# The last residual sum of a transformer kernel prepared ahead, and its last token tile worked in two column halves

## The chip, the cores and the metric

One core of a Trainium2 chip runs the kernel. The metric is the time of one execution on the device in microseconds (us), quoted as the median of several runs. Each run also has a state, fast or slow. PE is TensorE, DVE is VectorE, ACT is ScalarE, POOL is GpSimd, SP is SyncE, which here only issues transfers. The span is the time from the first to the last instruction in a trace. The views round it to 0.1 us; where this text gives the end of a span to 0.01 us, the figure is from the packed trace, which keeps it to the ns (1245.400 us before).

## The reference

Two layers, each a sliding-window attention and a feed-forward block (FFN), on x of 2048 tokens by 1024 columns in bfloat16. What matters here is the end of each FFN:

```python
def _B_ref(x, w1, b1, w2, b2):
    h = jnp.einsum("bsd,df->bsf", x, w1) + b1      # 1024 -> 3584
    h = _gelu(h)
    return jnp.einsum("bsf,fd->bsd", h, w2) + b2   # 3584 -> 1024
...
x = x + _B_ref(_layernorm(x, axis=-1), B_w1, B_b1, B_w2, B_b2)
```

## The kernel before

The tokens are worked in four groups of 512, so two layers make N = 8 groups of work. A group has four token tiles of 128 tokens. The second GEMM of the FFN, `gen_ffn2`, works the 1024 output columns in two halves (`dh`) of 512. For each it adds up 28 matmuls per token tile in one float32 tile `acc` of the matmul accumulator memory (six such tiles in rotation), in four steps `kq` of seven. After the last step of a token tile DVE makes two additions, first acc + b2, then + x, and in the second layer the tile goes to the output:

```python
def gen_ffn2(n):
    ...
    for dh in range(2):
        pss = [acc_tile() for _ in range(NTT)]
        for kq in range(4):
            wt = wpool.tile([P, KQ, HALF], BF16, name="wt")
            sp.dma_start(wt[:], w2_v[...])
            for tt in range(NTT):
                for k in range(KQ):
                    mm(pss[tt][:], lhsT=hT[:, kq * KQ + k, tt * P:(tt + 1) * P], rhs=wt[:, k, :],
                       start=(kq == 0 and k == 0), stop=(kq == 3 and k == KQ - 1))
                if kq == 3:
                    t = g * NTT + tt
                    xs = x[t][:, dh * HALF:(dh + 1) * HALF]
                    tmp = iop.tile([P, HALF], F32, name="tmp")
                    vec.tensor_tensor(out=tmp[:], in0=pss[tt][:], in1=b2bc[:, dh * HALF:(dh + 1) * HALF], op=ALU.add)
                    vec.tensor_tensor(out=xs, in0=tmp[:], in1=xs, op=ALU.add)
                    if l == NLAYER - 1:
                        sp.dma_start(out_v[t * P:(t + 1) * P, dh * HALF:(dh + 1) * HALF], xs)
                yield
```

The last stages of the program are `gen_wo` of groups 6 and 7 (the output projection of attention, with its residual and the normalization after it), then for both groups `gen_ffn1` and `gen_ffn2`. So x of group 7 is final three GEMMs, some 140 us, before its `gen_ffn2` begins.

## Time and profile before

| What | Value | Where it is read |
|---|---|---|
| time | 1247.13 us (1247.12 to 1247.34, 3 runs) | runs |
| PE busy | 1232.9 us, 99% of the span | page, busy time |
| last matmul ends | about 1240.9 us | timeline |
| two additions after it | 1240.98 to 1242.40 us, 1.42 us | timeline |
| last store issued, end of span | 1242.43 us, 1245.4 us | timeline |

The busy time of each engine (first line) and the chain that ended last (second and third), from the page of the kernel before:

```profile
PE 1232.9 (99%) x5757; PEld 627.9 (50%) x5807; DVE 836.5 (67%) x863; ACT 305.7 (25%) x475; POOL 97.7 (8%) x215
...
PE 78%; DVE 0%; issue 0%; POOL 0%; DVEq 0%
PE acc L118 78%; PE L L118 0%; DVE x L93 0%; DVE tmp L93 0%; POOL rstd L93 0%; DVE xn L93 0%; DVEq L93 0%
```

PE bounds the kernel. Other engines can only add time where PE waits for them, and at the very end, when PE is done. That end is this part of the timeline of the kernel before (start, duration, engine, line, operation, out<-in, shapes, count, and in brackets the idle time before it and its releaser):

```profile
1224.78 16.14 PE L118 MATMUL acc<-wt,hT 128*128 128x512 bf16 x72
...
1236.42 0.69 DVE L93 TENSOR_TENSOR tmp<-acc,b2bc 128x512 f32<-128x512 f32 x1 [18.19 <-PE acc L118]
...
1237.86 4.89 SPq L93 DMA_DIRECT2D out_dram<-x  x4
...
1239.46 0.69 DVE L93 TENSOR_TENSOR tmp<-acc,b2bc 128x512 f32<-128x512 f32 x1
1240.19 0.69 DVE L93 TENSOR_TENSOR x<-tmp,x 128x512 bf16<-128x512 f32 x1
1240.98 0.69 DVE L93 TENSOR_TENSOR tmp<-acc,b2bc 128x512 f32<-128x512 f32 x1
1241.71 0.69 DVE L93 TENSOR_TENSOR x<-tmp,x 128x512 bf16<-128x512 f32 x1
...
1242.43 0.33 SPq L93 DMA_DIRECT2D out_dram<-x  x1
```

Three things are to be seen. The last matmul ends at 1224.78 + 16.14 = 1240.92 us (matmul ends are modelled). Two additions of 0.69 us follow one another after it. And the additions of token tile 2, at 1239.46 and 1240.19, end at 1240.88, so DVE came free just before the last tile was ready: a token tile costs DVE 1.42 us and PE 1.51 us. The first SP line merges four store issues. The last line is the last of them alone, from a cut of the timeline that begins at 1241.4 us: it was issued at 1242.43 us, and the span ended 2.97 us later.

### The profile page before, as it was taken

Reading aid. Unit: us, or ns where it says so; the run is one execution under the profiler, and the core shown is the slowest. Engines: PE = TensorE matmul, PEld = TensorE weight load, DVE = VectorE, ACT = ScalarE, POOL = GpSimd, SP = SyncE. Lnnn points to the kernel's source line nnn. Section 1 sums busy time; section 2 is a strip of 40 time slices with the busy share of each in tenths; the row PEclk is TensorE's granted clock in tenths of the full one; section 3 lists DMA queues with packets and bytes.
Section 4 is the critical chain, followed back from the end, with each engine's and each line's share of the span. In section 5 each row is a group of like instructions: output and inputs, shape, how many; then the busy total and the mean of one; then the engine's idle time right before and its main releaser. Section 6 shows DMA issues by size and latency. Waiting matters only on the chain.

```text
span 1245.4 us, 13928 instructions
## 1 busy us (share of the span) xinstructions
PE 1232.9 (99%) x5757; PEld 627.9 (50%) x5807; DVE 836.5 (67%) x863; ACT 305.7 (25%) x475; POOL 97.7 (8%) x215
## 2 busy tenths in 40 slices
PE   8999999999999999999999999999999999999998
PEld 5666544446444564445644456444654444444443
DVE  4999989896995999427993379943598786011002
ACT  3333252013430134201341013510234001300310
POOL 3040010012001100101000010000001001000000
PEclk9999999999999999999999999999999999999999
DMA  9755564466846546655556575556654558446441
GB/s 278 262 187 169 153 207 148 161 176 204 215 132 205 167 154 201 191 170 149 177 170 196 166 184 166 162 199 197 182 168 132 186 198 202 157 157 194 156 143 39
DMA packets 215151, 219.81 MB, mean 176 GB/s; under 512 B 66018, under 2 KB 184816, under 8 KB 212016
## 3 DMA queue, kind: packets, MB, share of 16 engines
q1 hardware_dynamic: 212416, 208.16, 55.1%
q0 software_dynamic: 2672, 10.76, 2.6%
q8 instruction: 45, 0.74, 0.2%
q14 instruction: 18, 0.15, 0.0%
HBM read 197.40 MB, written 6.29 MB: 164 GB/s over the span
## 4 chain that ended last, share of the span: by engine, by line
PE 78%; DVE 0%; issue 0%; POOL 0%; DVEq 0%
PE acc L118 78%; PE L L118 0%; DVE x L93 0%; DVE tmp L93 0%; POOL rstd L93 0%; DVE xn L93 0%; DVEq L93 0%
## 5 line engine op out<-in xcount | busy, mean ns | idle before, releaser
L118 PE MATMUL acc<-xnT,wt 128*128 128x512 bf16 x3328 | 722.2, 379 | 1.1 <-ACT vT L93 0.7
L118 PEld LDWEIGHTS <-wt 128*128 128x128 bf16 x3328 | 394.7, 119 | 325.3 <-issue 5.3
L118 PE MATMUL acc<-wt,hT 128*128 128x512 bf16 x1752 | 386.0, 379 | 2.1
L118 PEld LDWEIGHTS <-hT 128*128 128x128 bf16 x1792 | 175.3, 98 | 211.5
L93 DVE TENSOR_TENSOR big<-big 128x2048 bf16<-128x2048 bf16 (+2 forms) x182 | 240.3, 1349 | 1.7
L93 ACT ACTIVATE hT<-acc,b1T 128x512 bf16<-128x512 f32 x224 | 151.7, 687 | 318.3 <-PE acc L118 317.7
L93 DVE TENSOR_TENSOR tmp<-acc,b2bc 128x512 f32<-128x512 f32 x64 | 44.1, 690 | 271.6 <-PE acc L118 267.5
L93 DVE TENSOR_TENSOR big<-abc,vT 128x4096 bf16<-128x4096 bf16 x64 | 144.2, 2282 | 49.3 <-DMA abc<-a_d 49.3
L93 DVE TENSOR_TENSOR big<-qT,kT 128x4096 bf16<-128x4096 bf16 x64 | 143.9, 2286 | 31.4 <-ACT kT L93 30.4
L93 ACT CAST qT<-acc 128x512 bf16<-128x512 f32 x64 | 37.2, 586 | 332.3 <-PE acc L118 332.2
L118 PE MATMUL acc<-wt,oT 128*128 128x512 bf16 x440 | 97.8, 379 | 1.1 <-DVE tmp L93 0.5
L93 DVE BATCH_NORM_STATS2 stats<-x 128x6 f32<-128x512 bf16 x128 | 84.2, 678 | 3.4 <-DMA x<-in_A_x_dram 2.5
L118 PEld LDWEIGHTS <-oT 128*128 128x128 bf16 x448 | 43.9, 98 | 53.9 <-issue 1.5
L93 ACT CAST vT<-acc 128x512 bf16<-128x512 f32 x64 | 37.5, 586 | 84.8 <-PE acc L118 84.8
L93 DVE TENSOR_SCALAR xn<-x,mv,rstd 128x1024 bf16<-128x1024 bf16 x64 | 34.8, 544 | 34.4 <-POOL rstd L93 30.0
L93 POOL TENSOR_TENSOR rstd<-mv,eps_t 128x1 f32<-128x1 f32 x64 | 17.6, 275 | 500.0 <-DVE mv L93 500.0
L93 ACT CAST kT<-acc 128x512 bf16<-128x512 f32 x64 | 37.4, 586 | 70.5 <-PE acc L118 70.5
L93 POOL DMA_DIRECT2D a_d<-a x32 | 19.6, 637 | 412.2 <-DVE a L93 412.2
L93 DVE TENSOR_TENSOR x<-tmp,x 128x512 bf16<-128x512 f32 x64 | 44.1, 690 | 1.8
L93 DVE TENSOR_TENSOR x<-acc,x 128x512 bf16<-128x512 f32 x64 | 42.7, 669 | 2.6 <-PE acc L118 2.3
L93 POOL TENSOR_TENSOR rstd<-rstd,mhalf 128x1 f32<-128x1 f32 x64 | 40.6, 634 | 5.0
L93 DVE TENSOR_TENSOR oT<-big 128x512 bf16<-128x512 bf16 x56 | 22.3, 415 | 0.2
(46 smaller groups left out, 179.4 us busy)
## 6 DMA issues: line engine op xcount, KB each, us to landing
wt<-in_B_w_dram SPq DMA_DIRECT2D x56, 1024.0 KB, 5.6
wt<-in_B_w_dram SPq DMA_DIRECT2D x64, 896.0 KB, 4.8
wt<-in_A_wqkv_dram SPq DMA_DIRECT2D x48, 1024.0 KB, 5.5
wt<-in_A_wo_dram SPq DMA_DIRECT2D x16, 1024.0 KB, 4.9
abc<-a_d POOLq DMA_DIRECT2D x32, 256.0 KB, 4.5
x<-in_A_x_dram SPq DMA_DIRECT2D x16, 256.0 KB, 6.1
out_dram<-x SPq DMA_DIRECT2D x32, 128.0 KB, 1.8
a_d<-a POOLq DMA_DIRECT2D x32, 64.0 KB, 3.6
```

Source lines behind the costliest of these rows:

```text
L93: inst = f(*args, **kwargs)
L118: return pe(nc.tensor.matmul(*args, **kwargs))
```

## The change

The intent is to have less to do after the last matmul. x + b2 of the last group is added up ahead in float32, so one addition is left per tile. The last token tile of the last column half is worked as two halves of 256 columns in two `acc` tiles, so the first half is added and stored while PE still works on the second.

```diff
+            xb2 = None
+            if n == N - 1:
+                xb2 = bigp.tile([P, NTT, HALF], F32, name="big")
+                for tt in range(NTT):
+                    vec.tensor_tensor(out=xb2[:, tt, :], in0=x[g * NTT + tt][:, cols], in1=b2bc[:, cols], op=ALU.add)
+
+            parts = [[slice(0, HALF)] for _ in range(NTT)]
+            if n == N - 1 and dh == 1:
+                parts[-1] = [slice(0, HALF // 2), slice(HALF // 2, HALF)]
+            pss = [[acc_tile() for _ in p] for p in parts]
...
-                    for k in range(KQ):
-                        mm(pss[tt][:], ...)
-                    if kq == 3:
...
+                    for ps, cs in zip(pss[tt], parts[tt]):
+                        ps = ps[:, 0:cs.stop - cs.start]
+                        for k in range(KQ):
+                            mm(ps, lhsT=hT[:, kq * KQ + k, tt * P:(tt + 1) * P], rhs=wt[:, k, cs],
+                               start=(kq == 0 and k == 0), stop=(kq == 3 and k == KQ - 1))
+                        if kq < 3:
+                            continue
+                        out_cols = slice(dh * HALF + cs.start, dh * HALF + cs.stop)
+                        xs = x[t][:, out_cols]
+                        if xb2 is not None:
+                            vec.tensor_tensor(out=xs, in0=ps, in1=xb2[:, tt, cs], op=ALU.add)
+                        else:
+                            ... the two additions as before ...
                         if l == NLAYER - 1:
-                            sp.dma_start(out_v[t * P:(t + 1) * P, dh * HALF:(dh + 1) * HALF], xs)
+                            sp.dma_start(out_v[t * P:(t + 1) * P, out_cols], xs)
```

In the compiled order the eight additions x + b2 move up to the last `gen_wo`, as soon as each x tile is final. The transposes of the last group move past a weight load in SP's queue.

More of the change, by code (lines that the diff above doesn't have):

```diff
@@ L397, in gen_ffn2 @@
         for dh in range(2):
-            pss = [acc_tile() for _ in range(NTT)]
+            cols = slice(dh * HALF, (dh + 1) * HALF)
+            xb2 = None
[6 more added lines that the diff above has]
+                parts[-1] = [slice(0, HALF // 2), slice(HALF // 2, HALF)]
@@ L399, in gen_ffn2 @@
+            pss = [[acc_tile() for _ in p] for p in parts]
             for kq in range(4):
                 wt = wpool.tile([P, KQ, HALF], BF16, name="wt")
-                sp.dma_start(wt[:], w2_v[:, kq * KQ:(kq + 1) * KQ, dh * HALF:(dh + 1) * HALF])
+                sp.dma_start(wt[:], w2_v[:, kq * KQ:(kq + 1) * KQ, cols])
                 for tt in range(NTT):
-                    for k in range(KQ):
-                        mm(pss[tt][:], lhsT=hT[:, kq * KQ + k, tt * P:(tt + 1) * P], rhs=wt[:, k, :],
-                           start=(kq == 0 and k == 0), stop=(kq == 3 and k == KQ - 1))
-                    if kq == 3:
-                        t = g * NTT + tt
-                        xs = x[t][:, dh * HALF:(dh + 1) * HALF]
-                        tmp = iop.tile([P, HALF], F32, name="tmp")
-                        vec.tensor_tensor(out=tmp[:], in0=pss[tt][:], in1=b2bc[:, dh * HALF:(dh + 1) * HALF], op=ALU.add)
-                        vec.tensor_tensor(out=xs, in0=tmp[:], in1=xs, op=ALU.add)
+                    t = g * NTT + tt
+                    for ps, cs in zip(pss[tt], parts[tt]):
[10 more added lines that the diff above has]
+                        else:
+                            tmp = iop.tile([P, HALF], F32, name="tmp")
+                            vec.tensor_tensor(out=tmp[:], in0=ps, in1=b2bc[:, out_cols], op=ALU.add)
+                            vec.tensor_tensor(out=xs, in0=tmp[:], in1=xs, op=ALU.add)
```

## The prediction

> **What bounds the kernel now.** TensorE. The page gives PE 1232.9 of 1245.4 us busy (99%) at full granted clock, and the chain of waits is PE `acc` matmuls nearly everywhere, but for the last microseconds. In the timeline the last matmul ends near 1240.92 us. After it come, in series: `tmp<-acc,b2bc` 0.69 us (from 1240.98), `x<-tmp,x` 0.69 us (until 1242.40), the last 128 KB store (issue 0.34 us, landing a median 1.8 us after it), and the end at 1245.4. The change can only shorten this tail of 4.5 us, of which two vector additions are 1.42 us.
>
> **What the change removes.** After the last matmul one 512-column addition goes, and the other shrinks to 256 columns. No duration for 256 stands in the trace. VectorE's float32 additions from PSUM take 0.69 us for 512 columns and 1.22 us for 1024, so 1.03 ns per column; estimate for 256: 0.43 us. The first half's addition is done by then: its matmuls end some 0.76 us before the last, and the addition of token tile 2 (0.69 us, acc ready 1.5 us before the end) is out of its way. So 1.42 us becomes 0.43 us: -0.99 us. The last store carries 64 instead of 128 KB, perhaps -0.1 us. The store before it is issued 0.8 us earlier, longer than an issue takes (0.34), so the queue should not hold it up.
>
> **What it adds.**
> - 28 matmuls of 512 columns become 56 of 256, with 28 more weight loads. The Trainium skill, "TensorE: Matmul & The Clock Gate", Back-to-back issue gap, gives 518 cycles for 512 columns and 262 for 256: 28 x 2.5 ns = 0.07 us (an estimate); the chain's 49 matmuls in 10.74 us (0.219 each, some records missing) agree with the first. The same section puts 128-column matmuls with weight loads at 81 ns apiece; this trace shows 8 transposes of 128 columns with 8 weight loads in 0.62 us, one lasting 0.22, so 57 ns apart. Such loads hide under 256-column matmuls of 109 ns: +0.07 us.
> - 8 additions `big<-x,b2bc` (0.4 to 0.7 us each, some 5 us of VectorE) run during the last wo stage (1033 to 1048 us), where VectorE already needs 3.64 us per token tile against PE's 3.46. VectorE falls some 3 us further behind. Six `acc` buffers of 1.73 us each give PE more slack than that, and the last group's `xnT` is not read until about 1150 us. Its transposes move relative to weight loads in the SP queue, but those loads are needed 20 us later. No PE stall: 0 us.
>
> **On the critical path:** -0.99 - 0.1 + 0.07, say -0.95 us of 1247.13, under 0.1%. Predicted 1246.2 us; 8 in 10 between 1245.6 and 1247.0. Faster by over 2%: 0.005; within 2%: 0.985; slower by over 2%: 0.01.
>
> **What would show each step right.** In the timeline after: one 256-column `x<-acc,big` of 0.43 us after the last matmul instead of two additions of 1.42 us; last matmul at 1240.9 to 1241.1 us; PE's `acc` waits on DVE still below 2 us in sum; the eight `big<-x,b2bc` between 1034 and 1058 us.
>
> **What would make it wrong.** Weight loads not hiding under 256-column matmuls (56 x 0.03 us = +1.5 us would eat the gain); PE waiting on VectorE or on a late weight tile in the last wo and the GEMM after it; the two last stores queueing behind each other; run-to-run differences of some tenths of a us.

## The result, and the profile after

The changed kernel took 1246.07 us (1245.99 to 1246.19, 6 runs), the kernel before 1247.18 us (1247.01 to 1247.34, 6 runs): 1.11 us less. The ratio is 0.9991 with a 95% interval of 0.9978 to 1.0004. A ratio is the mean time of one kernel's fast runs over that of the other's of the same rounds, so not quite the ratio of the medians quoted. The interval includes 1. Still, the six runs of one kernel and the six of the other do not overlap.

The end of the timeline of the changed kernel, in the columns of before (`big` is the tile that holds x + b2; the last line is again from a cut at 1241.4 us):

```profile
1224.78 16.19 PE L118 MATMUL acc<-wt,hT 128*128 128x512 bf16 x94
...
1236.45 0.69 DVE L93 TENSOR_TENSOR x<-acc,big 128x512 bf16<-128x512 f32 x1 [19.00 <-PE acc L118]
1237.17 4.62 SPq L93 DMA_DIRECT2D out_dram<-x  x5
1237.96 0.69 DVE L93 TENSOR_TENSOR x<-acc,big 128x512 bf16<-128x512 f32 x1 [0.82 <-PE acc L118]
1239.47 1.19 DVE L93 TENSOR_TENSOR x<-acc,big 128x512 bf16<-128x512 f32 x2 [0.82 <-PE acc L118]
1241.00 0.42 DVE L93 TENSOR_TENSOR x<-acc,big 128x256 bf16<-128x256 f32 x1 [0.34 <-PE acc L118]
...
1241.46 0.33 SPq L93 DMA_DIRECT2D out_dram<-x  x1
```

One addition of 0.42 us stands after the last matmul (1224.78 + 16.19 = 1240.97 us) where two stood, 1.42 us together. It ends at 1241.42 instead of 1242.40 us. DVE now waits for PE before it (0.34 us in the brackets), so it has no backlog. The last store is issued at 1241.46 us and the span ends at 1244.28, 2.82 us later against 2.97. So the additions gave 1.0 us and the smaller store some 0.15.

The work moved ahead lies in the last `gen_wo`. The kernel before, in its timeline: PE's matmuls of that stage, the first matmuls of the next, and the last addition of the stage:

```profile
1033.77 13.54 PE L118 MATMUL acc<-wt,qT 128*128 128x512 bf16 x61
...
1047.37 28.00 PE L118 MATMUL acc<-xnT,wt 128*128 128x512 bf16 x129
...
1048.93 0.68 DVE L93 TENSOR_TENSOR x<-acc,x 128x512 bf16<-128x512 f32 x1
```

The same in the kernel after, with the line of its first x + b2:

```profile
1033.53 13.76 PE L118 MATMUL acc<-wt,qT 128*128 128x512 bf16 x62
...
1037.99 0.68 DVE L93 TENSOR_TENSOR big<-x,b2bc 128x512 f32<-128x512 bf16 x1
...
1047.35 17.86 PE L118 MATMUL acc<-xnT,wt 128*128 128x512 bf16 x82
...
1051.05 0.68 DVE L93 TENSOR_TENSOR x<-acc,x 128x512 bf16<-128x512 f32 x1
```

DVE's last addition that frees an `acc` tile is 2.12 us later (1051.05 against 1048.93); only four of the eight x + b2 lie before it. The last normalization of the stage begins 3.39 us later (1054.91 against 1051.52 us), and the last x + b2 ends at 1056.66 us, in the next stage. PE begins the next GEMM at the same time. In the traces of all 14 kernels of this text, with none to eight sums ahead, 27.63 us lie between the first matmul of `gen_wo` of group 6 and the first of `gen_ffn1` of group 6. So the sums ahead cost PE nothing there. In the whole list of waits of the kernel after, PE's waits for DVE at `acc` in the lines of L118 are the ones below (sum, number, longest), 1.8 us together; the kernel before has the same three lines, and both have 1.2 us more at the transposes of L187, early in the program:

```profile
PE acc L118 <- DVE big L93: 1.1, 1, 1.1
PE acc L118 <- DVE tmp L93: 0.5, 1, 0.5
PE acc L118 <- DVE x L93: 0.2, 1, 0.2
```

### The profile page after: what moved, and what is told of

The parts are those of the page before. It is cut to its first block, busy times and chain, and to the rows that moved or that the text cites. A ratio compares the mean times of both kernels' runs of the same rounds, so it can differ in the third digit from the quotient of the medians.

```text
span 1244.3 us, 13978 instructions
## 1 busy us (share of the span) xinstructions
PE 1233.5 (99%) x5785; PEld 630.8 (51%) x5835; DVE 835.2 (67%) x864; ACT 305.7 (25%) x475; POOL 99.1 (8%) x215
## 4 chain that ended last, share of the span: by engine, by line
PE 79%; issue 0%; DVE 0%; POOL 0%
PE acc L118 78%; PE L L118 0%; DVE x L93 0%; POOL rstd L93 0%; DVE xn L93 0%
## 5 line engine op out<-in xcount | busy, mean ns | idle before, releaser
L118 PE MATMUL acc<-xnT,wt 128*128 128x512 bf16 x3328 | 722.1, 379 | 1.1 <-ACT vT L93 0.8
L118 PEld LDWEIGHTS <-wt 128*128 128x128 bf16 x3328 | 394.8, 119 | 325.2 <-issue 5.3
L118 PE MATMUL acc<-wt,hT 128*128 128x512 bf16 (+1 forms) x1780 | 386.0, 376 | 2.1
L118 PEld LDWEIGHTS <-hT 128*128 128x128 bf16 x1820 | 178.1, 98 | 209.0
L93 DVE TENSOR_TENSOR tmp<-acc,b2bc 128x512 f32<-128x512 f32 x56 | 38.6, 689 | 178.8 <-PE acc L118 175.4
L118 PE MATMUL acc<-wt,oT 128*128 128x512 bf16 x440 | 97.7, 379 | 1.1 <-DVE tmp L93 0.5
L118 PEld LDWEIGHTS <-oT 128*128 128x128 bf16 x448 | 43.9, 98 | 53.8 <-issue 1.3
L93 DVE TENSOR_TENSOR x<-acc,big 128x512 bf16<-128x512 f32 (+1 forms) x9 | 5.7, 632 | 90.0 <-PE acc L118 90.0
L93 DVE TENSOR_TENSOR x<-tmp,x 128x512 bf16<-128x512 f32 x56 | 38.6, 689 | 1.5
```

The source lines that it names most:

```text
L93: inst = f(*args, **kwargs)
L118: return pe(nc.tensor.matmul(*args, **kwargs))
```

## The experiments

Theory: only what DVE and the store still have to do after the last matmul counts. Rival A: DVE's additions in the last group count wherever they are. Rival B: the smaller last store is what gains. Beside these it was open whether the 28 more weight loads really hide, and whether the eight additions ahead cost anything. Each experiment ran five times, interleaved with the kernel before, in three sets of rounds on three chips (e1 to e4, e5 to e8, e9 to e12). All results were correct, and every 95% interval of a ratio to the kernel before was 0.12 to 0.14% to each side, some 1.6 us. So medians are compared with their ranges, and traces decide where medians differ by 0.2 us or less.

The table gives, besides the medians, four times read from each trace. The end of the last addition and the end of the span are counted from the start of the first addition of the last column half. Then comes the time from the last store's issue (read alone, by a narrow cut of the timeline) to the end of the span. The last column is the time from the first matmul of `gen_ffn1` of group 6 to the end of the span. Counting from a point that all kernels share drops what differs ahead of it: that matmul begins between 1047.25 us (e4) and 1047.60 us (e12), and `gen_wo` of group 6, ahead of the first instruction that the edits add or change, between 1019.62 and 1019.98 us in the same two. Each of these columns rests on one trace of each kernel.

| Kernel | median, range (us) | before, same rounds | last addition ends | span ends | issue to end | ffn1 to end |
|---|---|---|---|---|---|---|
| before | 1247.18, 1247.01 to 1247.34 | - | 5.98 | 8.98 | 2.97 | 198.03 |
| the change | 1246.07, 1245.99 to 1246.19 | 1247.18 | 4.98 | 7.82 | 2.82 | 196.93 |
| e1, sum ahead only | 1246.56, 1246.17 to 1246.62 | 1247.18 | 5.22 | 8.22 | 2.97 | 197.28 |
| e2, halves only | 1247.44, 1247.27 to 1247.63 | 1247.18 | 6.44 | 9.28 | 2.81 | 198.38 |
| e3, halves in two GEMMs | 1248.32, 1248.22 to 1248.42 | 1247.18 | 6.01 | 9.01 | 2.98 | 199.13 |
| e4, all but the last tile | 1247.09, 1246.96 to 1247.20 | 1247.18 | 5.95 | 8.95 | 2.97 | 198.00 |
| e5, sum for the last tile only | 1246.38, 1246.25 to 1246.53 | 1247.12 | 5.13 | 8.28 | 2.89 | 197.38 |
| e6, sum for the last two tiles | 1245.91, 1245.87 to 1246.03 | 1247.12 | 4.98 | 7.82 | 2.81 | 196.92 |
| e7, three pieces | 1246.18, 1245.77 to 1246.43 | 1247.12 | 4.86 | 7.85 | 2.69 | 197.01 |
| e8, one last store | 1246.16, 1246.01 to 1246.62 | 1247.12 | 4.97 | 7.97 | 2.97 | 197.08 |
| e9, e7 + ACT queue | 1245.88, 1245.71 to 1246.04 | 1247.18 | 4.86 | 7.62 | 2.73 | 196.78 |
| e10, e5 + ACT queue | 1246.26, 1246.26 to 1246.44 | 1247.18 | 5.12 | 8.05 | 2.89 | 197.15 |
| e11, the change + ACT queue | 1246.15, 1246.00 to 1246.37 | 1247.18 | 4.97 | 7.88 | 2.87 | 196.98 |
| e12, e6 + e9 | 1245.96, 1245.66 to 1246.07 | 1247.18 | 4.86 | 7.60 | 2.71 | 196.76 |

By the last column the change gained 1.10 us on the kernel before, and by the medians 1.11.

### e1: the sum prepared ahead, the last tile whole

```diff
-            if n == N - 1 and dh == 1:
-                parts[-1] = [slice(0, HALF // 2), slice(HALF // 2, HALF)]
```

> The prepared sum alone, last tile whole. Theory (only the vector work left after the last matmul counts): one 512-column addition of 0.70 us with its gap leaves the tail, so 0.72 us under the kernel before, about 1246.45 us, with 0.35 us still to gain from the halves. Rival A (VectorE work of the last group counts wherever it is): the full gain of the change, about 1246.1. Rival B (the gain comes from the smaller last store): no gain, 1247.2.

Measured 1246.56 us, 0.62 us under the kernel before; in the trace one addition of 0.69 us follows the last matmul. The theory had a gain of 0.72 us, and the last column has 0.75. Rival A would have had the full gain, rival B none. The halves add the remaining 0.49 us of the medians. By the last column it is 0.35 us: 0.25 from the shorter addition and 0.15 from the store, less 0.05 that the pairs ahead of the first addition cost (see e3).

### e2: the halves, with two additions each

```diff
-            if n == N - 1:
+            if False:
                 xb2 = bigp.tile([P, NTT, HALF], F32, name="big")
```

> The halves alone, each still with two additions. Naive reading (each half gains for itself): the last half costs two additions of 0.43 us after the last matmul instead of 1.42 us, so 0.5 us faster, about 1246.7. Theory with VectorE's backlog: token tile 2 keeps VectorE busy until the last matmul ends, so four additions of 0.43 us (1.75 us) follow it instead of two of 1.42 us in all: about 0.3 us slower in the tail, with 0.1 us given back by the smaller store and 0.07 us lost on TensorE: 1247.4 us.

Measured 1247.44 us: by itself this half of the change makes the kernel no faster, rather slower (0.35 us by the last column). The timeline of e2 shows why:

```profile
1240.15 0.69 DVE L93 TENSOR_TENSOR x<-tmp,x 128x512 bf16<-128x512 f32 x1
1240.94 0.42 DVE L93 TENSOR_TENSOR tmp<-acc,b2bc 128x256 f32<-128x256 f32 x1
1241.40 0.42 DVE L93 TENSOR_TENSOR x<-tmp,x 128x256 bf16<-128x256 f32 x1
1241.93 0.42 DVE L93 TENSOR_TENSOR tmp<-acc,b2bc 128x256 f32<-128x256 f32 x1
1242.39 0.43 DVE L93 TENSOR_TENSOR x<-tmp,x 128x256 bf16<-128x256 f32 x1
```

The first half is ready long before, but DVE is busy with token tile 2 until 1240.84. All four half additions then stand after the last matmul (it ends at 1240.89 us), and four of 0.42 us are more than two of 0.69: an addition costs 0.16 us whatever its width (by 0.424 us for 256 columns and 0.692 for 512; the 0.292 of e7 for 128 fit too). Here splitting pays only where the engine behind is free when the first part is ready, and it is the sum ahead that frees it.

### e3: 448 more pairs of weight load and matmul

The matmuls of the second GEMM of the last two groups in halves, on the kernel before; both halves of a tile in one `acc` tile.

```diff
-                    for k in range(KQ):
-                        mm(pss[tt][:], lhsT=..., rhs=wt[:, k, :], start=(kq == 0 and k == 0), ...)
+                    nh = 2 if n >= N - 2 else 1
+                    for h in range(nh):
+                        cs = slice(h * HALF // nh, (h + 1) * HALF // nh)
+                        for k in range(KQ):
+                            mm(pss[tt][:, cs], lhsT=..., rhs=wt[:, k, cs], start=(kq == 0 and k == 0 and h == 0), ...)
```

> The kernel before, with all matmuls of the second GEMM of the last two groups in halves of 256 columns (448 more pairs of weight load and matmul; sums and tail as before). Theory (a pair costs 2.5 ns, the weight load hides): 448 x 2.5 ns = 1.1 us slower, 1248.3 us. Rival (the weight load doesn't hide under 256 columns and costs some 30 ns a pair on 896 pairs): 27 us slower, 1274.

Measured 1248.32 us (1248.22 to 1248.42), 1.14 us over the kernel before: 1.14 us over 448 pairs is 2.5 ns each. The Trainium skill, "TensorE: Matmul & The Clock Gate", section Back-to-back issue gap, gives 262 cycles for 256 columns and 518 for 512, which makes an estimated 2.5 ns a pair at its 2.4 GHz; this run agrees. The weight loads hide, and 28 more pairs in the change cost 28 x 2.5 ns = 0.07 us. The traces of the other kernels show the same. From the first matmul of `gen_ffn1` of group 6 to the first addition of the last column half it takes 189.05 us where the last tile is whole (before, e1, e4). It takes 189.11 us where 21 more pairs lie in between (the change, for one), and 189.16 with 42 (e7, e9, e12): 0.05 us, or 2.5 ns a pair, each time.

### e4: the sum prepared for all tiles but the last

```diff
-                for tt in range(NTT):
+                for tt in range(NTT - dh):
                     vec.tensor_tensor(out=xb2[:, tt, :], ...)
...
-                        if xb2 is not None:
+                        if xb2 is not None and not (dh == 1 and tt == NTT - 1):
```

The halves are taken out too.

> The sum prepared for seven of the eight tiles of the last group; the last tile whole and by two additions as before. Theory (only what is left after the last matmul counts): nothing gained, 1247.2 us within 0.1. Rival A (VectorE work counts wherever it is): seven eighths of the gain of the prepared sums, about 1246.6.

Measured 1247.09 us: nothing, within the scatter (0.03 us in the trace). Seven of the eight prepared sums are worth nothing in themselves, and rival A falls.

### e5 and e6: the sum prepared for the last tile, or the last two

```diff
-            if n == N - 1:
+            if n == N - 1 and dh == 1:
                 xb2 = bigp.tile([P, NTT, HALF], F32, name="big")
-                for tt in range(NTT):
+                for tt in range(NTT - 1, NTT):      # e6: NTT - 2
...
-                        if xb2 is not None:
+                        if xb2 is not None and tt >= NTT - 1:      # e6: NTT - 2
```

> Halves, and the sum prepared for the last tile alone; token tile 2 by two additions. Theory with VectorE's backlog: tile 2 ends about when the last matmul does, so both half additions (2 x 0.43 us) follow it instead of one: 0.35 us slower than the change, about 1246.4 us. Without backlog: the same as the change, 1246.07.

> Halves, and the sum prepared for the last two tiles alone (two additions ahead instead of eight). Theory: the same tail as the change and so the same time, 1246.05 us within 0.1. Rival (the eight additions ahead cost time in the wo stage): faster than the change by the part that six additions cost, up to some tenths of a us. Rival A (VectorE work of the whole last group counts): slower, between 1246.5 and 1247.

e6, with two sums instead of eight, has the change's tail (7.82 us both), and its time (1245.91 us, 1.21 us under the kernel before of its rounds against 1.11) lies 0.16 us lower, which is within what runs scatter. So two of the eight additions carry the whole gain. The other six cost nothing that the traces show: the last column differs by 0.01 us.

e5's median, 1246.38 us, is what was expected, but in part by luck: by the last column it is 0.45 us behind the change instead of 0.35, and not for the reason given alone. These are DVE's last additions in e5 and, each from a narrow cut of its timeline, its last three store issues:

```profile
1240.17 0.69 DVE L93 TENSOR_TENSOR x<-tmp,x 128x512 bf16<-128x512 f32 x1
1240.78 0.75 DVE L93 TENSOR_TENSOR x<-acc,big 128x256 bf16<-128x256 f32 x2
```

```profile
1240.88 0.33 SPq L93 DMA_DIRECT2D out_dram<-x  x1
1241.31 0.38 SPq L93 DMA_DIRECT2D out_dram<-x  x1
1241.78 0.40 SPq L93 DMA_DIRECT2D out_dram<-x  x1
```

The backlog of token tile 2 cost only 5.13 - 4.98 = 0.15 us instead of 0.35, as two half additions that follow each other without a wait take 0.75 us together, and the first starts 0.08 us before the addition ahead of it has ended. But the last addition ended at 1241.53 us, and the last store was issued at 1241.78, some 0.25 us later; in the change it was 0.03 us. The three issues begin 0.43 and 0.47 us apart, each some 0.09 us after the one before has ended, and the two that had to wait last 0.38 and 0.40 us instead of 0.33. From the last issue to the end it was 2.89 us against 2.82 in the change. Together the queue cost 0.3 us.

### e7: three pieces of 256, 128 and 128 columns

```diff
-                parts[-1] = [slice(0, HALF // 2), slice(HALF // 2, HALF)]
+                parts[-1] = [slice(0, 256), slice(256, 384), slice(384, 512)]
```

> The last tile in three pieces of 256, 128 and 128 columns. Theory: the last addition has 128 columns, 0.29 us (estimate from 1.03 ns per column) instead of 0.42, the last store 32 KB, perhaps 0.05 us less; 28 more pairs cost 0.07 us on TensorE if the weight loads hide under 128 columns: 0.1 us faster than the change, about 1245.95. If a pair of 128 columns takes 81 ns instead of 57 (the skill's figure): 56 x 24 ns = 1.3 us slower, about 1247.3.

(The 81 ns are the skill's figure that the prediction names, and the 57 ns are from the trace of the kernel before.)

Measured 1246.18 us, 0.23 us over the expectation: not faster than the change, and not slower by 1.3 us. The end of the chain of e7 (start, duration, what), then, each from a narrow cut of its timeline, the last addition and the last three store issues:

```profile
1234.96 6.20 PE acc L118 x44
1241.16 0.02 issue
1241.18 0.29 DVE x L93
```

```profile
1241.18 0.29 DVE L93 TENSOR_TENSOR x<-acc,big 128x128 bf16<-128x128 f32 x1
```

```profile
1240.86 0.33 SPq L93 DMA_DIRECT2D out_dram<-x  x1
1241.28 0.41 SPq L93 DMA_DIRECT2D out_dram<-x  x1
1241.78 0.38 SPq L93 DMA_DIRECT2D out_dram<-x  x1
```

The addition came out as hoped, 0.29 us. Its end, counted from the first addition, is 4.86 us against 4.98: 0.12 us gained. PE lost no more than expected: DVE picked up token tile 2 at 1239.64 us and the last piece at 1241.18, 1.55 us later (1.546 in the packed trace), so 7 pairs of 256 columns (109 ns each) and 14 of 128 make 56 ns a pair of 128 columns. The loss is in the queue again: the last addition ended at 1241.47 us and its store was issued at 1241.78, 0.31 us later. By the last column e7 is 0.08 us behind the change: 0.12 us gained by the addition and 0.13 by the smaller store, 0.28 lost in the queue and 0.05 in the pairs ahead.

### e8: the last tile stored whole

```diff
-                            sp.dma_start(out_v[t * P:(t + 1) * P, out_cols], xs)
+                            if len(parts[tt]) == 1:
+                                sp.dma_start(out_v[t * P:(t + 1) * P, out_cols], xs)
+                            elif cs.stop == HALF:
+                                sp.dma_start(out_v[t * P:(t + 1) * P, cols], x[t][:, cols])
```

> The change, but the last tile stored whole (128 KB) after its second half addition. Theory: the store's size is worth 0.1 us or less, so 1246.1 to 1246.2 us. Rival B (the smaller store is what gains): most of the gain goes, 1246.8 or more.

Measured 1246.16 us. Rival B falls: with the large store nearly all of the gain stays. In the trace the last store is issued 2.97 us before the end (1244.48 us), as in the kernel before, against 2.82 in the change. The smaller store is worth 0.15 us, and the last column says the same (197.08 against 196.93).

```profile
1241.51 0.33 SPq L93 DMA_DIRECT2D out_dram<-x  x1
```

### e9 to e12: the last store from ScalarE's queue

ScalarE has nothing to do at the end, and its own queue can issue a store.

```diff
+                            last = n == N - 1 and dh == 1 and tt == NTT - 1 and cs.stop == HALF
-                            sp.dma_start(out_v[t * P:(t + 1) * P, out_cols], xs)
+                            (act if last else sp).dma_start(out_v[t * P:(t + 1) * P, out_cols], xs)
```

e9 is e7 with this, e10 is e5 with it, e11 the change with it, and e12 has the three pieces, the sum prepared for two tiles, and this. The expectations of e9 and e10 put the last issues of e7 and e5 at 1241.84 and 1241.85 us, and issues 0.49 us apart, because the author took three merged issues to last 0.33 us each. Read one by one, the last began at 1241.78 us in both, and issues 0.42 to 0.50 us apart.

> Three pieces as in e7, the last store issued by ScalarE's queue instead of SyncE's. Theory (in e7 the last addition ended at 1241.47 us and its store was issued at 1241.84, because three issues on one queue stood 0.49 us apart): 0.35 us under e7, about 1245.8 us, and 0.1 to 0.2 under the change. Rival (e7 lost its gain on TensorE, in pairs of 128 columns, or in landing of short rows): no better than e7, 1246.2.

> e5 (sum prepared for the last tile alone) with the last store from ScalarE's queue. Theory: e5 also lost 0.32 us because its last store waited for the queue (addition ended 1241.53, issue 1241.85); so about 1246.1 us, 0.3 under e5, leaving 0.15 us for the backlog of VectorE. Rival (the backlog is all of e5's loss): 1246.4 as in e5.

> Control: the change with the last store from ScalarE's queue. Theory: in the change the last store did not wait for the queue (addition ended 1241.42, issued by 1241.46), so nothing is gained: 1246.07 within 0.1. If ScalarE's queue is quicker in itself: clearly under 1245.9; if its first use costs: above 1246.2.

> Candidate for the best: three pieces, sum prepared for the last two tiles alone, last store from ScalarE's queue. Theory: the same tail as e9, so the same time within 0.1 us, about 1245.8.

The store of e9 in its timeline, at once after the last addition (1241.12 + 0.29 = 1241.41 us):

```profile
1241.44 0.38 ACTq L93 DMA_DIRECT2D out_dram<-x  x1
```

The same store in e10, whose last addition ended at 1241.62 us:

```profile
1241.64 0.37 ACTq L93 DMA_DIRECT2D out_dram<-x  x1
```

The wait for the queue is gone in both. By the last column e9 gained 0.23 us on e7, and e10 as much on e5; by the medians 0.30 and 0.12 (e10 was expected lower, at 1246.1). e12 lies within 0.1 us of e9, as expected. The control e11 gained nothing, so ACT's queue is not quicker in itself: in its trace the last issue is 2.87 us before the end against 2.82 in the change, and an issue lasts 0.37 us where SP's lasts 0.33. By the last column e9 and e12 are the shortest of all, 0.15 and 0.17 us under the change, and their medians are 0.19 and 0.11 us lower. These are the best versions that were found, at 1.2 to 1.3 us under the kernel before. That they beat the change rests on one trace of each, not on the times, whose ranges overlap. The times do not tell them from e6 either, which needs neither the third piece nor the second queue and lies 1.21 us under the kernel before of its rounds.

## Why the prediction was right

Measured 1246.07 us against 1246.2 predicted, and 1.11 us gained against 0.95.

- "So 1.42 us becomes 0.43 us: -0.99 us." Right: 1.42 became 0.42 us. The estimate from 512 and 1024 columns held at 256.
- "The first half's addition is done by then." Right, and e2 and e5 show that it hangs on token tile 2's own single addition: where that tile takes two, DVE still works on it when the last matmul ends.
- "The last store carries 64 instead of 128 KB, perhaps -0.1 us." A little small: 0.15 us by the traces of the change and of e8 (2.97 against 2.82 us).
- "+0.07 us" for PE. Right: e3 measured 2.5 ns a pair, and the traces of the change have 0.05 us for the 21 pairs ahead of the first addition. (The counter-case, 56 x 0.03 us, is 1.7 us and not 1.5.)
- "VectorE falls some 3 us further behind." Right at the end of the stage: 3.39 us at the last normalization. At the last addition that frees an `acc` tile it was 2.12 us, as only four of the eight additions lie before it. The x + b2 additions last 0.63 to 0.69 us, but the next starts before they have ended (1037.99, then 1038.58). The conclusion, no PE stall, held: the two `gen_wo` take 27.63 us with and without the sums.
- "longer than an issue takes (0.34), so the queue should not hold it up." Right in its conclusion, as the two last issues stood 0.77 us apart, but the yardstick was too short: issues that wait for the queue begin 0.42 to 0.50 us apart. In e5 and e7, where the pieces came closer together, the queue cost 0.3 us.
- Of the sum: from the last matmul to the end of the last addition it was 1.48 us and became 0.46, so -1.02 - 0.15 + 0.07 = -1.10 us stands against 1.11 measured. Of the 0.16 us by which the prediction was short, 0.07 is its own rounding (its terms make -1.02, and it said -0.95), 0.05 the store and 0.03 the additions.

## What to carry to other kernels

When one engine is busy 99% of the time, look at what remains after its last instruction, and count only that; the same work saved earlier bought nothing here (e4). Splitting the last tile shortens the tail only if every engine behind it keeps up with the pieces: here the additions first had to be halved in number, and at three pieces the issue of the stores became the limit, which a second queue lifted. At this size of effect (0.1% of the time) read the tail from traces, as five runs of each kernel do not tell 0.2 us apart. Count it from the last point that the kernels share: what lay ahead of it differed by up to 0.35 us between these traces, and that before anything edited had run. And read issues one by one: three merged into one line hide when the last began.

## What the Trainium skill lacked or had wrong

- "TensorE: Matmul & The Clock Gate", Back-to-back issue gap, gives 81 ns for a 128-column matmul and 131 ns for a 512-column one in a stream of weight load and matmul pairs, and calls N/2.4 + 2.5 the gap of isolated matmuls. Here a real kernel's stream follows the latter: 1.51 us per 7 pairs of 512 columns (216 ns), 109 ns at 256 (e3: 1.527 us per 14 pairs), and 56 ns at 128 (e7).
- "VectorE: DVE Perf Modes", The TRN2 errata: its fit (N + 151) / 0.96 ns for float32 additions, stated there for 512 and 2048 columns, also holds here for narrow ones with one operand in the accumulator memory: 424 ns measured at 256 columns (formula 424), 292 at 128 (formula 291), 692 at 512 (formula 691). Its table row of 120 + N cycles for such operands would give 392 ns at 256 columns, too little.
- "DMA: Bandwidth & Descriptors", Issuing engines are not separate DMA queues, says that a second issuing engine only saves issue time, usually small beside the transfer. That section gives no spacing for SP's stores: issues that wait for the queue begin 0.42 to 0.50 us apart here and show as 0.38 to 0.41 us (0.33 where none waits), and at the end of a kernel the second queue was worth 0.23 us (e10 against e5, e9 against e7).
- "DMA: Bandwidth & Descriptors", Anatomy of one DMA, fits 2.0 us and bytes over 436 GB/s for the GpSimd path alone. The last stores on SP's queue landed 1.7 us after their issue with 128 KB and 1.6 us with 64 or 32 KB, and from the last issue to the end of the span it was 2.97 us with 128 KB (2.97 to 2.98 over five kernels), 2.81 to 2.89 with 64 and 2.69 with 32.
